# Moving key transposes, block loads and two kinds of weight sums in a fused mLSTM and quick-GELU kernel

## The chip, the core and the metric

The kernel runs on one core of a Trainium2 chip. The metric is the device time of one execution in microseconds (us). This kernel scatters by about 1%. Below, "span" is the profiled execution from first to last instruction, some 1.7 us less than its device time (494.1 of 495.81 us for the kernel before).

## The reference

```python
# mLSTM cell: B=4, H=8, S=768, D=40; per head, for t in range(S):
m_new  = maximum(f[t] + m, i[t])
C      = exp(f[t] + m - m_new) * C + exp(i[t] - m_new) * outer(v[t], k[t])
n      = exp(f[t] + m - m_new) * n + exp(i[t] - m_new) * k[t]
y[t]   = sigmoid(o[t]) * (C @ q[t]) / maximum(abs(n @ q[t]), 1)
# the heads side by side: x (3072 tokens, 320), then
h = x @ w_in                        # 320 -> 2048
g = h * sigmoid(1.702 * h)
out = g @ w_out                     # 2048 -> 320
```

## The kernel before

The sequence is cut into six chunks of 128 positions (512 tokens over the batch). While TensorE runs the two large products of chunk `w`, the other engines prepare attention for chunk `w + 1` and loads run for `w + 2`. From the second chunk on, each large product is a Strassen-Winograd scheme: seven half-size products instead of eight. It needs sums of weight halves, made once (`first_sums` for the first product, `weight_sums` for the second), and sums of token halves in every chunk. All loads and stores go through one queue, SP.

Names in the traces: `k_bl` and `q_bl` are the buffers for the block loads, `kT` and `qT` the transposed keys and queries, `p_s` the scores made of them, `p_c` a chunk's new state, `p_u` and `p_v` the outputs of the first large product, `p_out` those of the second, `o_sb` an output tile on its way to the store. TensorE's outputs lie in banks, and the program writes a bank again only when VectorE or ScalarE has copied or added it out (in the kernel before TensorE stood 2.3 us for one such copy, `p_out` L610 for `o_sb` L613). "Columns" are the small transposes (L286) with which TensorE begins the next chunk's attention.

The parts that the change and the argument touch ("..." marks cuts):

```python
op = ctx.enter_context(tc.tile_pool(name="op", bufs=2))          # two output tiles
...
def load_blocks(w, which=slice(0, 2)):     # keys, then queries, of chunk w in 32x32 blocks: 32 DMAs
    ...
def transposes(w, b):                      # VectorE: kT from k_bl, qT from q_bl; frees k_bl, q_bl
    ...
def first_sums():                          # VectorE, 128x1024 each
    V.tensor_tensor(out=as1, in0=a10, in1=a11, op=OP.add)
    V.tensor_tensor(out=as2, in0=as1, in1=a00, op=OP.subtract)
    V.tensor_tensor(out=as4, in0=a01, in1=as2, op=OP.subtract)
    V.tensor_tensor(out=a10, in0=a00, in1=a10, op=OP.subtract)

def up_fast(w, j, between=None):           # half of a chunk's first product
    ...
    if j == 0:
        ...                                # VectorE: four token sums (L501 to L504) into bt1, bt2, b01, bt4
    if between:
        between()                          # next_keys
    ...
    product(chain, 0, a00, b00, True)      # TensorE: six of the seven products
    take(0, 0)
    product(other, 0, a01, b10, True)
    product(chain, 0, as2, bt2)            # the third needs the token sums
    ...
    product(other, 1, as4, b11)
    product(chain, 0, a10, b01)
    ...
    product(chain, 1, as1, bt1)
    for k in js:
        add(k, 0, 1, chain, 1)             # VectorE: the first adds (L521)
    for k in js:
        for i, p in enumerate((other, chain)):
            ...                            # TensorE (L541): writes the bank that the add reads
...
def weight_sums(n):                        # VectorE, 128x1280; n = 2: t4, needed from the second chunk's block 5
    ...
def next_keys():
    gates(w + 1)
    if w > 1:
        transposes(w + 1, 0)
        transposes(w + 1, 1)

for w in range(NW):
    ...
            if w and j == 3:
                for b in range(2) if w == 1 else range(2, 4):
                    transposes(w + 1, b)
    ...
    for i, block in enumerate(blocks):     # down blocks: the second product, mixed with attention of w + 1
        if w == 0:
            ...
            if i == 2:
                first_sums()
            for b in {2: (0, 1), 7: (2,), 9: (3,)}.get(i, ()):
                transposes(1, b)
        elif w == 1 and i in (2, 3):
            transposes(2, i)
        if w and w + 2 < NW and i == (4 if w == 1 else 0):
            load_gates(w + 2)
            load_blocks(w + 2)
        block()                            # its last part: copy or add to an output tile, store
        ...
        elif i in (12, 14, 15):
            weight_sums((12, 14, 15).index(i))
    if w == 0:
        load_blocks(2)
```

## Time and profile before

| Kernel before | value |
|---|---|
| median of the first three runs | 497.21 us (496.63 to 500.64) |
| span of the profiled run, granted clock | 494.1 us, 0.993 |
| TensorE / VectorE / ScalarE busy | 483.8 / 342.9 / 221.2 us |
| first product to first product, second chunk (118.74 to 200.29) | 81.55 us |
| the same, third chunk (200.29 to 276.58) | 76.29 us |

The second chunk does the same work as the third and takes 5.3 us more; that is the simplest sign of where something is to be had. A mean clock of 0.993 is worth reading too: a stretch of about 3.4 us at half clock (here 81.8 to 85.2 and 187.6 to 191.0 us) takes 0.0035 off the mean of a 494 us span, so 0.993 says "two such stretches".

The lines that the argument rests on are in the prediction.

### The profile page before, as it was taken

Reading aid. Unit: us, or ns where it says so; the run is one execution under the profiler, and the core shown is the slowest. Engines: PE = TensorE matmul, PEld = TensorE weight load, DVE = VectorE, ACT = ScalarE, POOL = GpSimd, SP = SyncE. Lnnn points to the kernel's source line nnn. Section 1 sums busy time; section 2 is a strip of 40 time slices with the busy share of each in tenths; the row PEclk is TensorE's granted clock in tenths of the full one; section 3 lists DMA queues with packets and bytes.
Section 4 is the critical chain, followed back from the end, with each engine's and each line's share of the span. In section 5 each row is a group of like instructions: output and inputs, shape, how many; then the busy total and the mean of one; then the engine's idle time right before and its main releaser. Section 6 shows DMA issues by size and latency. Waiting matters only on the chain. (4 is left out here: it accounts for less than half of the span.)

```text
span 494.1 us, 10439 instructions
## 1 busy us (share of the span) xinstructions
PE 483.8 (98%) x4076; PEld 399.2 (81%) x4076; DVE 342.9 (69%) x855; ACT 221.2 (45%) x575; POOL 62.9 (13%) x103
## 2 busy tenths in 40 slices
PE   8999998999999988999999999999999999999997
PEld 5874365777778988877999977999977999877897
DVE  8788769797678927586686576786666776344841
ACT  6766676211558400474900364920255930155400
POOL 4030002232000330000232000142000030000000
PEclk9999998999999998999999999999999999999999
DMA  8999799403697360696300397400095000000000
GB/s 129 179 275 346 102 264 179 43 14 67 77 179 161 47 89 4 103 252 81 33 30 1 76 263 80 53 15 16 31 245 84 1 1 29 27 2 0 1 27 28
DMA packets 175953, 44.87 MB, mean 91 GB/s; under 512 B 164352, under 2 KB 169504, under 8 KB 175904
## 3 DMA queue, kind: packets, MB, share of 16 engines
q1 hardware_dynamic: 175904, 44.21, 47.6%
q8 instruction: 32, 0.52, 0.4%
q14 instruction: 17, 0.14, 0.1%
HBM read 40.17 MB, written 4.01 MB: 89 GB/s over the span
## 5 line engine op out<-in xcount | busy, mean ns | idle before, releaser
L400 ACT COPY xT<-p_x 128x384 f32<-128x384 f32 x24 | 11.0, 481 | 134.8 <-PE p_x L399 134.8
L610 PE MATMUL p_out<-w_out_sb,g 128*128 128x160 f32 x480 | 70.7, 303 | 0.0
L610 PEld LDWEIGHTS p_out<-w_out_sb,g 128*128 128x128 f32 x480 | 67.4, 192 | 0.9
L521 DVE TENSOR_TENSOR g<-p_u,g 128x256 f32<-128x256 f32 x80 | 34.0, 425 | 47.0 <-PE p_u L513 37.0
L518 ACT COPY g<-p_u 128x256 f32<-128x256 f32 x120 | 43.1, 378 | 42.8 <-PE p_u L513 38.6
L525 ACT ACTIVATE g<-g 128x256 f32<-128x256 f32 x120 | 42.4, 426 | 39.1 <-DVE g L521 39.1
L337 POOL TENSOR_SCALAR_AFFINE_SELECT wt<-wt 128x1024 f32<-128x1024 f32 x20 | 23.0, 1152 | 230.8 <-ACT wt L335 230.8
L615 DVE TENSOR_TENSOR o_sb<-o_sb,p_out 128x160 f32<-128x160 f32 x70 | 21.3, 316 | 41.7 <-PE p_out L610 41.3
L335 ACT ACTIVATE wt<-wt,cols 128x128 f32<-128x128 f32 x160 | 47.9, 390 | 0.0
L513 PE MATMUL p_u<-xT,w_in_sb 128*128 128x256 f32 x160 | 38.9, 382 | 0.0
L610 PE MATMUL p_out<-t,big 128*128 128x160 f32 x240 | 36.3, 305 | 2.3 <-DVE o_sb L613 2.3
L513 PE MATMUL p_u<-xs,big 128*128 128x256 f32 x160 | 37.9, 380 | 0.3 <-issue 0.3
L561 PE MATMUL p_out<-w_out_sb,g 128*128 128x320 f32 x128 | 37.7, 450 | 0.0
L541 PE MATMUL p_v<-xT,w_in_x 64*128 64x512 f32 x80 | 37.0, 602 | 0.0
L541 PE MATMUL p_u<-xT,w_in_x 64*128 64x512 f32 x80 | 37.0, 602 | 0.0
L610 PEld LDWEIGHTS p_out<-t,big 128*128 128x128 f32 x240 | 34.0, 193 | 2.6 <-DVE o_sb L613 2.4
L350 DVE TENSOR_TENSOR wt<-p_s,wt 128x512 f32<-128x512 f32 x48 | 30.4, 681 | 7.5 <-POOL wt L337 5.6
L513 PEld LDWEIGHTS p_u<-xs,big 128*128 128x128 f32 x160 | 29.9, 190 | 5.3 <-issue 0.7
L513 PEld LDWEIGHTS p_u<-xT,w_in_sb 128*128 128x128 f32 x160 | 29.6, 190 | 5.4 <-DVE o_sb L615 1.5
L561 PEld LDWEIGHTS p_out<-w_out_sb,g 128*128 128x128 f32 x128 | 24.7, 197 | 10.8 <-issue 1.7
L521 DVE TENSOR_TENSOR g<-p_v,g 128x256 f32<-128x256 f32 x80 | 29.8, 414 | 0.0
L541 PEld LDWEIGHTS p_v<-xT,w_in_x 64*128 64x128 f32 x80 | 14.2, 186 | 17.4 <-issue 17.4
(168 smaller groups left out, 865.0 us busy)
## 6 DMA issues: line engine op xcount, KB each, us to landing
wt<-m_row SPq DMA_DIRECT2D x20, 512.0 KB, 7.0
out_dram<-o_sb SPq DMA_DIRECT2D x24, 160.0 KB, 1.8
eo<-in_o_gate_dram SPq DMA_DIRECT2D x5, 640.0 KB, 6.0
v_st<-in_v_dram SPq DMA_DIRECT2D x5, 640.0 KB, 8.9
k_st<-in_k_dram SPq DMA_DIRECT2D x5, 640.0 KB, 11.2
big<-in_moe_w_in_dram SPq DMA_DIRECT2D x5, 512.0 KB, 6.6
k_bl<-in_k_dram SPq DMA_DIRECT2D x40, 64.0 KB, 2.8
q_bl<-in_q_dram SPq DMA_DIRECT2D x40, 64.0 KB, 2.8
```

What stands on the lines that cost most here:

```text
L335: A.activation(out=x[:, h, :], in_=x[:, h, :], func=AF.Exp, scale=-1.0, bias=cols[w][:, b * H + h:b * H + h + 1])
L337: G.affine_select(out=x, in_=x, compare_op=OP.is_ge, fill=0.0, base=0, pattern=[[0, H], [1, L]], channel_multiplier=-1)
L350: V.tensor_tensor(out=wt[w, b][:, :, i, :], in0=pw[i], in1=wt[w, b][:, :, i, :], op=OP.mult)
L400: A.copy(out=xT[w][:, :, b, :], in_=px)
L513: T.matmul(p[k][:, ts[t]], a[:, k // 2, k % 2 * 128:(k % 2 + 1) * 128], b, start=first, stop=True, skip_group_check=True)
L518: A.copy(out=g[k][i][:, ts[t]], in_=chain[k][:, ts[0]])
L521: V.tensor_tensor(out=g[k][i][:, ts[t]], in0=p[k][:, ts[pt]], in1=g[k][i][:, ts[t]], op=OP.add)
L525: A.activation(out=dst, in_=dst if src is None else src, func=AF.Gelu_apprx_sigmoid)
L541: T.matmul(p[k], w_in_x[r, k, :], x[r, 2, :], start=False, stop=True, skip_group_check=True)
L561: T.matmul(po, gs[w, f // 2][:, f % 2, b * L:(b + 1) * L], w_out_sb[:, f, :], start=(f == 0), stop=(f == NF - 1))
L610: T.matmul(po, a(f), b[:, f, :], start=(f == 0), stop=(f == NH - 1))
L615: V.tensor_tensor(out=dst, in0=x, in1=po, op=OP.add)
```

## The change

Its intent is to give the second chunk the order of instructions that the later ones have: two of the four first sums move from the first chunk into the second chunk's first product, the third chunk's key blocks are loaded ahead of the first chunk's stores so that the transposes can also be done in that product, the fourth chunk's blocks can then be loaded earlier, and the third weights' sum goes to where there is time for it.

```diff
-    def first_sums():
-        ... four sums
+    def first_sums(ns):
+        for n in ns:
+            ... sum n of the same four
...
     def next_keys():
+        if w == 1:
+            first_sums((2, 3))
         gates(w + 1)
-        if w > 1:
-            transposes(w + 1, 0)
-            transposes(w + 1, 1)
+        transposes(w + 1, 0)
+        transposes(w + 1, 1)
...
                 if w and j == 3:
-                    for b in range(2) if w == 1 else range(2, 4):
+                    for b in range(2, 4):
                         transposes(w + 1, b)
...
                 if i == 2:
-                    first_sums()
+                    first_sums((0, 1))
+                if i == 10:
+                    load_blocks(2)
                 for b in {2: (0, 1), 7: (2,), 9: (3,)}.get(i, ()):
                     transposes(1, b)
-            elif w == 1 and i in (2, 3):
-                transposes(2, i)
-            if w and w + 2 < NW and i == (4 if w == 1 else 0):
+            elif w + 2 < NW and i == 0:
                 load_gates(w + 2)
                 load_blocks(w + 2)
             block()
...
+            if w == 1 and i == 1:
+                weight_sums(2)
...
-            elif i in (12, 14, 15):
-                weight_sums((12, 14, 15).index(i))
-        if w == 0:
-            load_blocks(2)
+            elif i in (12, 14):
+                weight_sums(i // 2 - 6)
```

More of the change, by code (lines that the diff above doesn't have):

```diff
@@ L483 @@
     as1, as2, as4 = (big[:, i, :].rearrange("p (n m) -> p n m", m=256) for i in (4, 5, 3))
-    def first_sums():
-        V.tensor_tensor(out=as1, in0=a10, in1=a11, op=OP.add)
-        V.tensor_tensor(out=as2, in0=as1, in1=a00, op=OP.subtract)
-        V.tensor_tensor(out=as4, in0=a01, in1=as2, op=OP.subtract)
-        V.tensor_tensor(out=a10, in0=a00, in1=a10, op=OP.subtract)
+    def first_sums(ns):
+        for n in ns:
+            out_, in0, in1, f = ((as1, a10, a11, OP.add), (as2, as1, a00, OP.subtract), (as4, a01, as2, OP.subtract),
+                                 (a10, a00, a10, OP.subtract))[n]
+            V.tensor_tensor(out=out_, in0=in0, in1=in1, op=f)
     def up_fast(w, j, between=None):
```

## The prediction

> **What bounds the kernel now.** I read the page first: TensorE is busy 98% of a span of 494.1 us, VectorE 69%. So only what makes TensorE wait, or run slow, can move the time; 98% also says how little there is. The second view is the list of TensorE's waits:
>
> ```profile
> PE p_out L610 <- DVE o_sb L613: 2.3, 1, 2.3
> PE p_s L348 <- DVE qT L302: 1.9, 1, 1.9
> ...
> PE p_out L610 <- DVE o_sb L615: 1.0, 2, 0.6
> ...
> PE p_u L513 <- issue: 0.3, 1, 0.3
> ```
>
> Columns: who waited for whom, us in total, times, longest. The reader is to see that two single waits, 2.3 and 1.9 us, are nearly all, each one event, each ended by VectorE. Third, TensorE's timeline around both, and the same place one chunk later as a yardstick:
>
> ```profile
> 80.93 1.35 PE L348 MATMUL p_s<-qT,kT 40*128 40x128 f32 x16 [1.86 <-DVE qT L302]
> ...
> 182.48 1.39 PE L425 MATMUL p_c<-v_st,k_st 128*40 128x41 f32 x64
> 186.14 3.28 PE L610 MATMUL p_out<-t,big 128*128 128x160 f32 x16 [2.26 <-DVE o_sb L613]
> 189.21 3.22 PE L610 MATMUL p_out<-w_out_sb,g 128*128 128x160 f32 x16
> ...
> 263.62 1.39 PE L425 MATMUL p_c<-v_st,k_st 128*40 128x41 f32 x64
> 264.95 2.44 PE L610 MATMUL p_out<-t,big 128*128 128x160 f32 x16
> 267.23 2.34 PE L610 MATMUL p_out<-w_out_sb,g 128*128 128x160 f32 x16
> ```
>
> After the wait the same 16 matmuls take 3.28 and 3.22 us, against 2.44 and 2.34 a chunk later. Fourth, a table of windows shows why:
>
> ```profile
> 82.20:85.80 3.60, 3.60 (x10) 2.46 (x9) 3.23 (x6) 0.94 (x2) 0.00 (x0) 0.59 1.05 296
> ...
> 186.20:191.20 5.00, 5.00 (x25) 5.00 (x26) 4.69 (x15) 0.00 (x0) 0.24 (x1) 0.66 0.01 3
> ```
>
> The granted clock (third column from the end) is 0.59 and 0.66 behind the two waits, 1.00 nearly everywhere else. A wait is paid twice: once idle, once slow. Fifth, VectorE's timeline says what held it at each place:
>
> ```profile
> 76.40 1.23 DVE L488 TENSOR_TENSOR big<-w_in_sb,big 128x1024 f32<-128x1024 f32 x1
> 77.55 2.11 DVE L489 TENSOR_TENSOR w_in_sb<-w_in_sb 128x1024 f32<-128x1024 f32 x1
> 79.58 0.70 DVE L302 STREAM_TRANSPOSE kT<-k_bl 128x512 f32<-128x512 f32 x1
> 80.21 0.66 DVE L302 STREAM_TRANSPOSE qT<-q_bl 128x512 f32<-128x512 f32 x1
> ...
> 185.53 0.56 DVE L613 COPY o_sb<-p_out 128x160 f32<-128x160 f32 x2 [9.40 <-DMA out_dram<-o_sb]
> ```
>
> At 79 us the transposes come behind the four first sums. At 185 us VectorE stood 9.40 us for an earlier store of its own output tile, of which there are two. Sixth, the DMA queue says why that store was late:
>
> ```profile
> 109.27 8.74 SPq L566 DMA_DIRECT2D out_dram<-o_sb  x4
> 118.07 9.27 SPq L117 DMA_DIRECT2D k_bl<-in_k_dram  x16
> 127.38 8.47 SPq L117 DMA_DIRECT2D q_bl<-in_q_dram  x16
> ...
> 165.16 8.93 SPq L117 DMA_DIRECT2D k_bl<-in_k_dram  x16
> 174.19 8.40 SPq L117 DMA_DIRECT2D q_bl<-in_q_dram  x16
> 183.02 15.65 SPq L619 DMA_DIRECT2D out_dram<-o_sb  x3
> ```
>
> There is one queue. The stores of the second chunk stand behind 32 block loads, 17.3 us of issuing, and these waited 9.2 us (the queue's own waits) for the last key transpose, at 164.44, that frees their buffer.
>
> [...] The trace has the half (0.50 from 82 to 85 and from 188 to 191 us), but after waits of only 1.86 and 2.26 us; the 0.31 us wait at 122.5 was followed by a clock of 1.00. [...] the two slow sums, 1.99 and 2.11 us, are those beside which GpSimd ran its masks (73.71 and 77.21).
>
> **The change part by part.** The order of instructions, compared between the two kernels, confirms that no engine gains or loses an instruction; all is movement.
>
> *Two sums leave the first chunk.* 1.23 + 2.11 = 3.3 us go from in front of the transposes at 79.58. But qT needs its block loads: the last is issued at 76.5 and lands 2.5 us later (time to landing of those issues), at 79.0. So qT starts at 79.0 and not 76.9, ends at 79.7, and TensorE, free at 79.06, waits 0.7 and not 1.86 us: 1.2 gained. If 0.7 us is too short to cost the clock (I think so), the slow stretch goes too: 16 down matmuls took 6.03 us there against 4.57 later, the scores 1.35 against 1.16, 1.65 together. Gain 2.8 us at 90 us.
>
> *Blocks ahead of the first chunk's stores.* They now start once the last key transpose is done (97.57 - 2.8, so 95.0) and take 9.0 + 8.5 us: issued at 112.5. The first store, ready at 106, then goes at 112.5 and lands 2.4 us later (as that at 183.02 did), at 114.9. The third output copy, due at 115.15 - 2.8 = 112.35, waits for it: a new VectorE wait of 2.5 us. From there to the token sums (L501) were 6.65 us; the weights' sum that has moved away saves 1.41 and the wait for GpSimd 0.66: 114.9 + 4.6 = 119.5, before 121.8. TensorE, which would be there 2.8 earlier, needs these for its third product, at about 120.4 instead of 122.78. 0.4 is given back: 2.4 left.
>
> *The second chunk's start.* VectorE now does token sums 1.47, two weights' sums (GpSimd idle, so 1.2 each) 2.4, gates 2.4, four transposes 2.5 (204.67 to 207.16 in the third chunk): first add at 119.5 + 8.8 = 128.3. The sums are done at 122.2 and 123.4, for products due at 122.1 and 123.9: in time or 0.1 late. But TensorE, through six products at 129.85 - 2.4 = 127.4, needs the first add (0.4) at 128.7 before it may write that bank: a new stall of about 1.3 us, too short, I think, for the clock. Left: 1.1 us. Before, VectorE had 2.99 us of idle time there; it had neither sums nor transposes in it.
>
> *Second chunk's blocks at its first block.* The third chunk shows how this goes: block loads from 222.4 to 240.0, stores only at 255, no such wait. The transposes that held the buffer at blocks 2 and 3 are gone from there. So from p_c (182.48) to the next chunk's first product (200.29), 17.81 us should be the third chunk's 276.58 - 263.62 = 12.96: gain 4.85.
>
> *The third sum after block 1.* It adds 1.48 us where two transposes (1.3) leave, and is due only at block 5: nothing.
>
> Sum: 1.1 + 4.85 = 6.0 us. 497.2 - 6.0 = 491.2 us, 1.2% less.
>
> **The rivals.** (1) The first chunk gives nothing back: had VectorE enough slack at the turn, 2.8 + 0.3 + 4.85 = 8.0 us, 489.2. For it: the third to fifth chunks run the same gates and transposes there with 2.65 us to spare. Against: theirs start 0.4 us after TensorE's first product, here 3.5 us after, and with 2.4 us more. (2) The new waits cost the clock too, or that at 79 us, though shorter, still does: 1.7 us each, so 492.9 with one and 494.6 with two. For it: 1.86 us was enough[...]. Against: 0.58 us at 192.4 was not. (3) The store wait is only moved, from 185 to 115 us, and holds TensorE as long: gain 2, 495. Against: at 185 the waiting copy itself released the two banks TensorE needed; at 115 four banks are in use and the next product comes 3.6 us after.
>
> **Range and chances.** The largest gain I can build is 8.5 us with the 0.7 us wait gone too, 488.7; the smallest likely is 2, 495. Range 488.7 to 495.0, predicted 491.2. Over 2% would need 9.9 us, as much as all idle time in the span (494.1 - 483.8 = 10.3): chance 0.04. Within 2%: 0.95. Slower by 2%: 0.01, as nothing is added.
>
> **What would show it.** In the changed profile: TensorE's wait for qT at 79 us under 1 us, released by a DMA at one remove, and the clock 1.00 from 82 to 86; a VectorE wait of 2 to 3 us of L565's copy for out_dram near 112; TensorE waiting 1 to 1.5 us for L521 near 127 to 129; no 9.4 us wait in the second chunk, clock 1.00 there, and 76.3 us from the third chunk's first product to the fourth's, as before, but some 77.5 for the second chunk, before 81.55. I am wrong if the clock stays at 0.5 behind any of these, if the second chunk keeps a store wait, or if the first add comes in time.

## The result, and the profile after

The changed kernel took 491.79 us (median of 6 runs, 489.52 to 493.79) against 497.69 us for the kernel before (6 runs, 495.62 to 500.64). The ratio is 0.9874, 95% interval 0.9827 to 0.9920; ratios here are the mean time of one kernel's runs over that of the other's in the same rounds, so not quite the ratio of the medians. Repeated on another chip it was 0.9899 (0.9867 to 0.9932). So 5 to 6 us less, against 6.0 predicted.

The profiled run of the changed kernel was in the slower half of its kind (492.45 us) and that of the kernel before a fast one (495.81 us), so the two traces differ by only 3.4 us. They are good for showing where, not for how much in all. TensorE's waits now:

```profile
PE p_s L348 <- DVE qT L302: 2.2, 1, 2.2
...
PE p_u L513 <- DVE o_sb L565: 0.4, 1, 0.4
PE p_out L610 <- DVE o_sb L615: 0.4, 1, 0.4
```

The 2.3 us wait for the second chunk's output copy is gone. The wait for qT, which was to shrink to 0.7 us, is 2.2 us. A 0.4 us wait for the first chunk's output copy is new. VectorE's timeline says why:

```profile
78.42 0.70 DVE L302 STREAM_TRANSPOSE kT<-k_bl 128x512 f32<-128x512 f32 x1
81.27 0.71 DVE L302 STREAM_TRANSPOSE qT<-q_bl 128x512 f32<-128x512 f32 x1 [2.15 <-DMA q_bl<-in_q_dram]
...
117.88 0.49 DVE L565 COPY o_sb<-p_out 128x320 f32<-128x320 f32 x1 [3.17 <-DMA out_dram<-o_sb]
...
122.15 0.42 DVE L501 TENSOR_TENSOR xs<-xT 128x256 f32<-128x256 f32 x1
...
124.76 1.22 DVE L489 TENSOR_TENSOR w_in_sb<-w_in_sb 128x1024 f32<-128x1024 f32 x1
...
130.88 1.42 DVE L521 TENSOR_TENSOR g<-p_u,g 128x256 f32<-128x256 f32 x4
```

The columns are start, duration, engine, line, operation, and in brackets the idle time before it and what ended it. VectorE came to the transposes 1.2 us earlier than before (78.42, before 79.58) and then stood 2.15 us for the query blocks: these set the start now. At 117.88 is the new wait for a store, 3.17 us, and behind it the token sums start at 122.15. The last sum, moved to where GpSimd is idle, takes 1.22 us instead of 2.11, when a mask of GpSimd (77.21 to 78.59) lay beside it. That the mask alone makes the difference is not shown: one that began at 73.71 lay partly beside the first sum too, and that took 1.22 us. TensorE at the same places:

```profile
82.04 1.16 PE L348 MATMUL p_s<-qT,kT 40*128 40x128 f32 x16 [2.23 <-DVE qT L302]
83.13 4.57 PE L561 MATMUL p_out<-w_out_sb,g 128*128 128x320 f32 x16
...
118.21 1.56 PE L513 MATMUL p_u<-xT,w_in_sb 128*128 128x256 f32 x6
120.22 0.70 PE L513 MATMUL p_u<-xT,w_in_sb 128*128 128x256 f32 x2 [0.44 <-DVE o_sb L565]
...
130.27 1.12 PE L541 MATMUL p_v<-xT,w_in_x 64*128 64x512 f32 x2
131.36 0.69 PE L541 MATMUL p_u<-xT,w_in_x 64*128 64x512 f32 x1
...
183.96 1.39 PE L425 MATMUL p_c<-v_st,k_st 128*40 128x41 f32 x64
185.29 2.44 PE L610 MATMUL p_out<-t,big 128*128 128x160 f32 x16
```

Four readings. The 16 down matmuls behind the qT wait take 4.57 us, before 6.03: no slow stretch, though the wait was longer than before (an estimate of why is under "All four sums back"). The second chunk's first product breaks off after six of eight matmuls for the fourth bank. The matmul that must wait for the first add starts at 131.36, 1.1 us behind its partner at 130.27. And p_c is followed by the next product at once, at 2.44 us instead of 3.28. The clock behind the qT wait, in a table of windows (third column from the end):

```profile
82.10:87.60 5.50, 5.50 (x32) 3.88 (x32) 5.17 (x10) 1.28 (x5) 0.00 (x0) 1.00 1.18 239
```

The DMA queue:

```profile
68.41 10.90 SPq L117 DMA_DIRECT2D q_bl<-in_q_dram  x16
...
97.07 8.81 SPq L117 DMA_DIRECT2D k_bl<-in_k_dram  x16
105.98 9.50 SPq L117 DMA_DIRECT2D q_bl<-in_q_dram  x16
115.58 4.94 SPq L566 DMA_DIRECT2D out_dram<-o_sb  x4
...
155.97 8.54 SPq L117 DMA_DIRECT2D q_bl<-in_q_dram  x16
175.67 22.13 SPq L619 DMA_DIRECT2D out_dram<-o_sb  x4
```

The second chunk's query blocks are issued from 68.41 us (66.25 before). The picture of the second chunk before has moved to the first chunk: its first store, ready at 108.7, goes at 115.58 behind 32 block loads. In the second chunk the block loads end at 164.5 and the first store at 175.67 meets an empty queue.

For the bookkeeping I cut each trace at three points that every variant has: the second chunk's columns' transpose (near 68 us), that chunk's first product, its second half (the first product of `j == 4`), and the third chunk's first product. Start to columns varies by 0.9 us over the fourteen traces, and from the third chunk on all take the same time.

| us | A: columns to first product | of it, wait for qT | B: first half of first product | C: second half to next chunk | A+B+C |
|---|---|---|---|---|---|
| before | 50.94 | 1.86 | 16.58 | 64.97 | 132.49 |
| changed | 49.67 | 2.23 | 18.61 | 60.10 | 128.38 |
| changed, other chip | 48.72 | 1.28 | 18.96 | 60.10 | 127.78 |

So C gives 4.87 us, A gives 1.3 to 2.2, and B takes 2.0 to 2.4 back.

### The profile page after: what moved, and what is told of

Its sections match the earlier page's. It is cut to its first block, busy times and chain, and to the rows that moved or that the text cites.

```text
span 490.7 us, 10441 instructions
## 1 busy us (share of the span) xinstructions
PE 481.3 (98%) x4076; PEld 396.8 (81%) x4076; DVE 343.3 (70%) x855; ACT 221.3 (45%) x575; POOL 60.9 (12%) x103
## 5 line engine op out<-in xcount | busy, mean ns | idle before, releaser
L610 PEld LDWEIGHTS p_out<-w_out_sb,g 128*128 128x128 f32 x480 | 66.3, 190 | 0.9
L561 PE MATMUL p_out<-w_out_sb,g 128*128 128x320 f32 x128 | 36.2, 437 | 0.0
L561 PEld LDWEIGHTS p_out<-w_out_sb,g 128*128 128x128 f32 x128 | 23.9, 190 | 10.0 <-issue 0.5
L348 PE MATMUL p_s<-qT,kT 40*128 40x128 f32 x384 | 26.0, 281 | 2.2 <-DVE qT L302 2.2
```

The lines of the kernel that those rows point to most:

```text
L348: T.matmul(pw[i][:, p, :], kT[w, b][r, p, :], qT[w, b][r, p, :], start=True, stop=True)
L561: T.matmul(po, gs[w, f // 2][:, f % 2, b * L:(b + 1) * L], w_out_sb[:, f, :], start=(f == 0), stop=(f == NF - 1))
L610: T.matmul(po, a(f), b[:, f, :], start=(f == 0), stop=(f == NH - 1))
```

## The experiments

Two theories on the first part. Theory A: the landing of the query blocks sets the wait for qT, and the slow clock behind it comes or not by chance. Theory B: the split of the sums removes the slow clock. On the second part: VectorE is late at the start of the second chunk because of the store wait, or because of the amount of work put there. All ran on chip, all gave correct results, each beside runs of the kernel before on the same chip; the first four on one chip, the next four on a second, the last four on a third. The changed kernel itself ran only on the chip of the first result and on that of the first four: where a later kernel is set against it, the comparison goes through the kernel before.

**The changed kernel again**, no edit.

> The changed kernel once more, unaltered, on the chip of the next three. In its first profile TensorE still waited 2.2 us for qT, because the query blocks were issued 2.2 us later than in the kernel before, and yet the clock stayed at 1.00. Theory A (the block loads' landing sets that wait, and it moves by some 2 us from run to run[...]): the wait is again 0.7 to 2.5 us, released by a transpose that waited for the query blocks' transfer, the dip is there or not, and the second chunk's 9.4 us store wait is absent; ratio to before 0.985 to 0.991. Theory B (the split of the sums removes the slow clock for good): clock 1.00 behind the qT wait again, whatever its length.

Measured: 491.91 us, before 496.56; ratio 0.9899 (0.9867 to 0.9932). The wait for qT was 1.28 us, behind 2.0 us of VectorE waiting for the query blocks; no slow stretch in the trace, one in six runs by the clock counter (0.996). Both theories survive, but the wait of 1.3 to 2.2 us in two traces is not the 0.7 predicted.

**The split of the sums alone**, on the kernel before.

```diff
                 if i == 2:
-                    first_sums()
+                    first_sums((0, 1))
...
     def next_keys():
+        if w == 1:
+            first_sums((2, 3))
         gates(w + 1)
```

> The kernel before, with only the last two first-sums moved to the second chunk's first product (no blocks ahead, no transposes there, third weights' sum where it was). My prediction's step: 2.8 us gained at 90 us, none lost at the turn, because VectorE had 2.99 us idle there and gets 2.4 us of sums: ratio 0.994. Theory A (the wait for qT is set by the query blocks' landing): 0 to 1.2 us gained, ratio 0.997 to 1.000, with VectorE's qT transpose idle for the query blocks' transfer. Both: the 9.4 us store wait of the second chunk is still there, and no TensorE stall for the first add.

Measured: 494.62 us, ratio 0.9965 (0.9924 to 1.0006), so not told apart from no change. In the trace: A 49.00 (wait 1.55), B 16.64, C 65.44. A is 1.9 us shorter, VectorE waits 2.1 us for the query blocks, B is unchanged: the two sums fit into the idle time there, as predicted. C brought a surprise. TensorE's timeline, then the clock between the two waits:

```profile
184.92 2.44 PE L610 MATMUL p_out<-t,big 128*128 128x160 f32 x16 [2.72 <-DVE o_sb L613]
...
191.80 2.44 PE L610 MATMUL p_out<-t,xs 128*128 128x160 f32 x16 [2.27 <-DVE o_sb L615]
```

```profile
185.00:187.00 2.00, 2.00 (x15) 2.00 (x16) 1.97 (x7) 0.00 (x0) 0.00 (x0) 1.00 0.00 0
187.00:189.00 2.00, 2.00 (x17) 2.00 (x16) 1.79 (x7) 0.00 (x0) 0.00 (x0) 1.00 0.04 8
```

The second chunk's wait was followed by no slow stretch in this run, the clock stayed at 1.00, and yet p_c to the next chunk took 18.28 us, 0.47 more than with the slow clock before. The first wait was 0.46 us longer; without it both stretches are the same, 15.56 and 15.55 us. With the full clock TensorE only waits again, 2.27 us, at the next thing VectorE owes. After standing 9.8 us for the store VectorE has a backlog, and in these two traces this sets the end of that stretch, whatever TensorE's clock.

**The early blocks of the second chunk alone**, on the kernel before.

```diff
-            elif w == 1 and i in (2, 3):
-                transposes(2, i)
-            if w and w + 2 < NW and i == (4 if w == 1 else 0):
+            elif w == 1 and i == 0:
+                transposes(2, 2)
+                transposes(2, 3)
+            if w and w + 2 < NW and i == (1 if w == 1 else 0):
```

> The kernel before, with the third chunk's last two key transposes at the second chunk's first down block and the fourth chunk's block loads right behind, so that they are issued by about 174 us, ahead of the first store; nothing of the first chunk touched. If the gain is the second chunk's store wait and the slow clock behind it: the 9.4 us wait of the output copy is gone, p_c to the next chunk's first product is 13.0 us instead of 17.8, 4 to 5 us gained, ratio 0.990 to 0.992. If the gain comes from the first chunk's sums and transposes instead: under 2 us, ratio over 0.996.

Measured: 492.75 us, ratio 0.9907 (0.9868 to 0.9947). C is 60.41, so 4.56 us less; p_c to the next chunk 12.96. The output copy waits 0.8 us instead of 9.4, and TensorE does not notice:

```profile
178.69 0.56 DVE L613 COPY o_sb<-p_out 128x160 f32<-128x160 f32 x2 [0.79 <-DMA out_dram<-o_sb]
```

A was 52.13 with a qT wait of 3.04 us and a slow stretch, by far the worst of the traces, and B 16.58 as before. This one part gives nearly all that the whole change gives.

**Output tiles of their own for the first chunk**, on the changed kernel. Two more tiles do not fit (the pool wants 5 KB per partition where 2.875 are left), so the third and fourth copies borrow the room of the third weights' sum, which the change leaves unused until the second chunk.

```diff
-            o = op.tile([128, DM], FP, tag="o", name="o_sb")
+            if b < 2:
+                o = op.tile([128, DM], FP, tag="o", name="o_sb")
+            else:
+                o = t4.rearrange("p a b -> p (a b)")[:, (b - 2) * DM:(b - 1) * DM]
             V.tensor_copy(out=o, in_=po)
```

> The changed kernel, with the third and fourth output tile of the first chunk in the room of the third weights' sum (unused until the second chunk), so that those copies need not wait for the stores behind the block loads. If that wait (3.2 us) is what makes VectorE late at the second chunk's start: the wait of L565 for out_dram is gone, the token sums start some 2.5 to 3 us earlier, TensorE's 0.4 us wait for the fourth bank and most of its 2 us loss in the first half product go, 1.5 to 2.5 us less than the changed kernel, ratio to before 0.982 to 0.985. Rival (the sums and transposes themselves overfill the time before the first add): under 0.7 us less.

Measured: 487.79 us, ratio 0.9834 (0.9794 to 0.9874); 4 us less than the changed kernel on the same chip. B fell to 16.41, 2.2 to 2.6 us less, as the first theory has it; in all it is more than the 1.5 to 2.5 us expected. Part of the rest is the qT wait, 0.59 us in this trace, which the edit does not touch: A + B + C is 124.54, 3.2 us less than on the same chip without the edit. The wait of the copy for a store is gone.

**The query blocks earlier**, on the changed kernel.

```diff
+                if w == 0 and j == 2:
+                    load_blocks(1, 1)
                 if j == 4:
-                    if w == 0:
-                        load_blocks(1, 1)
```

and the conversion of one weight piece (16) moved from step 5 to step 7 of the list of conversions.

> The changed kernel, with the second chunk's query blocks issued one pair of products earlier in the first chunk, ahead of two weight fetches (and the piece that one of them brings converted two blocks later). Theory A (the landing of the query blocks, not the sums, sets what is left of TensorE's wait for qT, 0.6 to 2.2 us in three profiles): VectorE's wait for the query blocks, 2 us, and TensorE's for qT are both gone or under 0.3 us; from the columns' transpose to the second chunk's first product 47.4 us or a little less; 0.6 to 2 us less than the changed kernel, unless VectorE's store wait takes it back: then the first half product grows by as much. Theory B (the transposes are late for another reason, VectorE's backlog of conversions): the wait stays over 1 us.

Measured: 490.15 us, ratio 0.9839 (0.9816 to 0.9863). TensorE's line, with no wait:

```profile
78.86 1.16 PE L348 MATMUL p_s<-qT,kT 40*128 40x128 f32 x16
```

A is 47.62. Theory A holds for the wait: in the traces with two sums in the first chunk, A less the wait was 47.44 (changed, both chips; 48.03 - 0.59 with own tiles) and now nearly all of A is that. One thing expected did not come: VectorE still stands in front of its qT transpose, 4.97 us instead of 2 (ended, by the profile, by a weight fetch issued just behind the query blocks), since with the conversion moved it is done with the sums 6 us earlier. But qT starts at 77.35, and TensorE comes for it at 78.86: only TensorE's wait counts. B stayed at 18.71. The clock was 0.999 to 1.000 in all six runs.

**The transposes later**, on the changed kernel.

```diff
     def next_keys():
...
-        transposes(w + 1, 0)
-        transposes(w + 1, 1)
+        if w > 1:
+            transposes(w + 1, 0)
+            transposes(w + 1, 1)
...
-                    for b in range(2, 4):
+                    for b in range(4) if w == 1 else range(2, 4):
                         transposes(w + 1, b)
```

> The changed kernel, with the third chunk's first two pairs of transposes taken out of the second chunk's first product and put with the others after its first half (four pairs there, 2.6 us more, before 2.2 us of idle time). The store wait of the third output copy stays. If VectorE's amount of work before the first add makes the stall, and the store wait only adds to it: the first half product takes 18.6 to 19.0 - 2.0 = about 16.8 us, the second half 0.3 to 0.5 more than 15.9, ratio to the kernel before 0.984 to 0.987. If the store wait alone makes the loss, through TensorE's wait for the fourth bank and late token sums: still over 18 us.

Measured: 491.45 us, ratio 0.9860 (0.9828 to 0.9892). B was 17.56: half way between what the two theories expected. The store wait was still there (3.2 us), as was TensorE's 0.48 us wait for the fourth bank. So of B's loss of 2.0 to 2.4 us, 1.0 to 1.4 go with the transposes, and what is left above the 16.41 of the kernel with own tiles, 1.15, stays with the store wait, through the bank and the late token sums. Neither theory alone holds: both make the loss. With the store wait away the transposes cost little: 16.41 there, against 16.02 in the next kernel, which has neither.

**No early blocks in the first chunk**: the kernel before with the split sums, the edit of the second chunk's blocks and the later third sum, so that the third chunk's blocks stay behind the first chunk's stores.

> The kernel before with the split sums, the later third weights' sum, and the fourth chunk's blocks at the second chunk's second down block with its transposes just ahead (as in blocks_alone), but the third chunk's blocks still behind the first chunk's stores. No store waits in either chunk: first to second half product 16.4 us, p_c to the next first product 13.0, what is left is the wait for qT: about as fast as the changed kernel with tiles of its own, ratio 0.982 to 0.986. If the early blocks are what the gain hangs on: no better than blocks_alone, 0.990.

Measured: 488.77 us, ratio 0.9813 (0.9785 to 0.9841). A 48.84 (wait 1.39), B 16.02, C 60.42. On its chip that is 1.9% below the kernel before; the changed kernel was 1.3 and 1.0% below on its two. The gain does not hang on the early blocks: without them B is the shortest of all, and no store holds the first chunk's copies.

**Own tiles and early query blocks together**, both edits as above on the changed kernel.

> The changed kernel with output tiles of their own in the first chunk and the query blocks issued earlier: all three waits taken away. Expected: no TensorE wait over 0.5 us after the first 20 us, clock 1.00 in nearly every run, 486.0 to 487.5 us, ratio 0.979 to 0.982. If the query blocks' transfer, moved ahead, delays the weights' conversion instead: a new wait of VectorE or ScalarE for a weight fetch between 66 and 90 us and no gain over tiles of its own alone (0.983).

Measured: 488.88 us, ratio 0.9813 (0.9785 to 0.9841). A 47.55, B 16.41, C 60.10, no wait over 0.5 us behind the start-up, clock 1.000 in six of six runs. The time expected, 486.0 to 487.5, was missed by the median: three runs at 487.6 to 487.9, three at 489.8 to 490.6. The trace is of a run of the lower group; what the others did is not known.

**All four sums back**, on the changed kernel: the split undone, everything else left.

> The changed kernel with all four first sums back in front of the second chunk's transposes; blocks ahead of the stores, transposes at the first product and the later third weights' sum stay. Profiles so far: kernels with four sums there took 49.1 us from the columns' transpose to the next chunk's first product beside the wait for qT, those with two 47.44, the difference being a stretch of halved clock. If the split is what keeps the clock (theory B), this kernel has the slow stretch again: clock near 0.997 in most runs, about 49.1 plus a wait of 1.8 to 3 us, while its first half product is 1.0 to 1.5 us shorter than the changed kernel's 18.6 to 19.0, as 2.4 us of VectorE work left it: together 1 to 2 us slower than the changed kernel. If the clock's dip is chance (theory A): dips in some runs only, as for the changed kernel in 2 of 12, and about as fast.

Measured: 491.94 us, ratio 0.9906 (0.9883 to 0.9930), the changed kernel's time and not the 1 to 2 us more that theory B expected. A was 51.09 with a wait of 2.0 us, so 49.1 beside it, 1.65 more than the 47.44 without a slow stretch; B 17.18. The slow stretch is there:

```profile
82.00:84.00 2.00, 2.00 (x12) 1.45 (x9) 1.46 (x3) 0.00 (x0) 0.00 (x0) 0.50 1.13 237
```

Counting by the runs' mean clock (0.997 or less): with four sums in the first chunk and no second-chunk store wait, 10 of 12 runs had a slow stretch (this kernel and blocks_alone); with two, 9 of 40 (the changed kernel twice, own tiles twice, transposes later, no early blocks, third sum back); with early query blocks, 0 of 16. So theory B is right that the split mostly keeps the clock, A that it is not certain.

The kept traces say more, though no run was made to test it. The traces record when the granted clock changes. In the kernel before the recorded changes are 22, 1, 30, 1 and 89 steps of 3.413 us apart (the clock fell at 81.76 and 187.58 us and came back 3.41 us after each), in the changed kernel two changes are 142 such steps apart, and the steps lie elsewhere than in the kernel before. Take it that the steps also go on between the recorded changes: this is an estimate from these change times, as nothing in the traces marks a step where the clock does not change. The table says how much of each of TensorE's waits then lay in one step; for the blocks alone and the four sums back, the steps are laid by the times at which the clock of the windows falls and returns (near 83.2 and 86.6, 81.9 and 85.3 us).

| trace, wait | length, us | most of it in one step, us (estimate) | granted clock after it |
|---|---|---|---|
| blocks alone, qT | 3.04 | 2.60 | half |
| four sums back, qT | 2.02 | 2.02 | half |
| before, second chunk's output copy | 2.26 | 1.98 | half |
| before, qT | 1.86 | 1.86 | half |
| changed, qT | 2.23 | 1.19 (and 1.04) | full |
| sums alone, second chunk's outputs | 2.27 and 2.72 | not known | full |
| third sum back, token sums | 1.60 | 1.60 or less | full |

All other waits behind the start-up were at most 1.64 us long, and the clock stayed full. So the length of a wait alone does not decide in these traces: 1.86 us was followed by the half clock, and 2.23, 2.27 and 2.72 us were not. By the estimate it is how much of the wait falls into one step, 1.86 us or more in the four that were followed by the half clock against 1.19 us in the changed kernel's; where the border lies is not shown. The split keeps the clock, in most runs, by shortening the wait; at some 2 us the half clock came in one trace (2.02) and not in another (2.23).

What the split gives in A, it takes back in B, 1.4 to 1.8 us, because VectorE is behind there.

**The third weights' sum back**, on the changed kernel: `weight_sums(2)` again behind the first chunk's last block.

> The changed kernel with the third weights' sum back behind the last block of the first chunk, in front of the token sums. VectorE is behind there, so its 1.4 us should be paid in full: the first half product 20.0 to 20.4 us instead of 18.6 to 19.0, 1.0 to 1.5 us slower than the changed kernel, ratio 0.990 to 0.993. If VectorE's lateness at the first add is not what counts there: no change, 0.987 to 0.990.

Measured: 492.39 us, ratio 0.9949 (0.9908 to 0.9990). B was 20.70, 1.7 to 2.1 us longer, a little more than expected, and the ratio is above the 0.990 to 0.993 expected. The copy waited 3.87 us for a store here, and TensorE stood 1.10 us for the fourth bank and 1.60 us for the token sums, which come behind this sum. In this run TensorE did not wait for qT at all; the two slowest runs (497.12 and 495.62) had two slow stretches each by the clock counter (0.993).

**No early blocks, early query blocks**: both edits as above.

> no_early_blocks with the query blocks issued earlier: no wait for qT, no store wait, and the shortest first half product (16.0 us). From its parts: 487.2 - 1.4 = 485.8 us span, some 0.5 to 1.4 us less than no_early_blocks, ratio 0.977 to 0.981, clock 1.00 in nearly all runs. If the earlier query blocks cost as much by delaying the weights: 0.981 as without.

Measured: 488.38 us, ratio 0.9839 (0.9811 to 0.9866), clock 1.000 in four of four runs. B 16.02, C 60.42, but A 48.32: the wait for qT is gone and a wait of 0.85 us for the second chunk's values, loaded behind the query blocks and the delayed weights, has come in its place. Expected 0.5 to 1.4 us better than without; on its own chip each is 1.6 to 1.9% below the kernel before, and the intervals overlap. The transfer only changed places with another.

**Own tiles once more**, on the last chip.

> The changed kernel with output tiles of its own in the first chunk, a second time, on the chip of the other three, so that the two ways around the store wait can be compared: first half product 16.4 us, wait for qT 0.6 to 2 us, ratio 0.981 to 0.985, 0.5 to 1.5 us slower than no_early_blocks_q.

Measured: 487.42 us, ratio 0.9830 (0.9801 to 0.9859): A 47.37 (no wait for qT), B 16.41, C 60.10. VectorE at the turn (with the edit's line numbers, three higher):

```profile
113.74 0.49 DVE L568 COPY t<-p_out 128x320 f32<-128x320 f32 x1
...
116.97 0.43 DVE L501 TENSOR_TENSOR xs<-xT 128x256 f32<-128x256 f32 x1
```

The token sums start at 116.97, 1.65 us after TensorE's first product at 115.32; in the changed kernel it was 3.94 (122.15 - 118.21). It was to be slower than no_early_blocks_q by 0.5 to 1.5 us and was 1.0 us faster by the median: the two ways around the store wait are not told apart. Either beats both kernels: 487.4 to 488.9 us for all of them, against 491.8 and 497.

## Why the prediction was right or wrong

The time (491.2, measured 491.8 and 491.9) and the verdict were right. By its steps:

*The second chunk's blocks.* Right, to the number: 12.96 us from p_c to the next chunk's product, 12.96 predicted, and 4.87 us in C for 4.85. The early blocks alone give 4.56 there. But the reading "a wait is paid twice: once idle, once slow" failed at this wait: the sums_alone trace has it without the slow clock and loses as much (18.28 us from p_c to the next chunk, against 17.81). It was VectorE's backlog, as that one pair of traces has it; the sum was right because it was taken from a whole stretch and not from the two terms.

*Two sums leave the first chunk.* The mechanism was right: the query blocks take over as what sets qT. The size was off. 0.7 us of wait, worked out from one trace's landing at 79.0 us, was 2.23 and 1.28 us, since in the other traces the same loads were issued up to 2.2 us later (68.41 against 66.25 for the first). This can be checked over all traces with the split and the loads in their old place: the six with a wait have the issue of the first query block, counted from the columns, plus 2.2 to 2.4 us (changed: 68.41 - 68.54 = -0.13, wait 2.23; own tiles: 66.18 - 67.93 = -1.75, wait 0.59), and the two where the issue came 2.8 and 3.0 us before the columns have none. With the issue of the kernel before, 66.25 - 67.80 = -1.55, this makes 0.7 to 0.9. So the step that failed is to take one trace's issue time for all. The clock staying up was right for most runs, but in the profiled one not for the reason given, a wait too short: it was 2.23 us long and yet the clock stayed full. By the estimate above a border between two steps cut it into 1.19 and 1.04 us, and that would be luck. Gain in A: 2.8 predicted, 1.3 and 2.2 measured.

*Blocks ahead of the first chunk's stores.* A new VectorE wait of 2.5 us was predicted at the right copy; it was 3.2 and 3.5. The loads began at 97.07 and not at 95.0, following the late transposes, and took 18.4 us for 17.5.

*The second chunk's start.* B was to grow by 1.7 us (2.8 less the 1.1 left); it grew by 2.0 and 2.4. The stall at the first add was 1.1 us for 1.3. What I had missed is TensorE's wait for the fourth bank, 0.44 and 0.81 us: in arguing against the third rival I said four banks were in use and the next product far off, but the last of its four outputs needs just the bank whose copy was late. The second chunk's length that I gave, 77.5 us, did not follow from these terms, which make 81.55 - 4.85 + 1.7 = 78.4; measured 78.7 and 79.1. (The largest gain in the range, too, is 8.65 us by its own terms and not 8.5; nothing hangs on it.)

*The third sum.* "Nothing" at its new place stands: C is the same 60.1 with it there and with it away (third_sum_back). That taking it from its old place matters was in the sum (1.41 us) and is shown: 1.7 to 2.1.

So two terms were too good, by 0.6 to 1.5 us in A and 0.3 to 0.7 in B, and the traces add up to 4.1 and 4.7 us where 6.0 was predicted. The runs give 6.3 and 5.0 by their ratios. The rest is within their scatter, and one part of it is known: the slow clock came in every run of the kernel before but one of 33, and in 2 of the changed kernel's 12. That the total fell so close is thus partly luck. Of the rivals, the first (8.0 us with nothing given back) is what the kernel reaches with its own output tiles, at 487.4 to 487.8 us: 8.8 and 9.3 us below the kernel before. What remains open is why the first loads differ by up to 3.5 us between runs (the second chunk's first query block was issued at 64.94 to 68.41 us in the kernels that issue it at the same place), and why three of the six runs with own tiles and early query blocks took 2 us more at a clock of 1.000.

## What to carry to other kernels

With all loads and stores on one queue, putting 32 block loads (18.4 us of issuing) ahead of the first chunk's stores moved the wait here to the copy that needed the store's buffer next (3.2 us); look for that buffer before you move loads, and for room lying idle to take its place. When an engine comes back from a long wait (here 9.4 us), price its whole backlog from a clean copy of the stretch (12.96 us against 17.81) rather than adding up single waits, and before you take the landing of a transfer from one trace, look at how it moves in a second (the wait for qT was 2.23 and 1.28 us in two runs of one kernel). And leave out the parts of a change one by one: here the loads moved ahead in the first chunk were not needed for the gain.
